# First loads handed to three DMA queues in another order, and matmuls on constants placed ahead of the first data

## The chip, the cores and the metric

The kernel runs on one core of a Trainium2 chip. A core has a matrix engine (TensorE, in the profile PE, with its weight loads as PEld), a vector engine (VectorE, DVE), a scalar engine (ScalarE, ACT), a general engine (GpSimd, POOL) and a sync engine (SyncE, SP) that issues most transfers. The metric is the device time of one launch in microseconds: the median of several runs, 953.85 us over 4 runs (952.91 to 955.61).

## The reference

A linear attention without softmax, normalised per head, feeds a two-layer network with a gated activation. All is float32 in value (the two weight matrices arrive as float64 and are converted in the kernel).

```python
# q, k, v: (8 batches, 8 heads, 576 tokens, 64); g_norm: (64,)
kv  = einsum('bhsd,bhse->bhde', k, v)            # one 64x64 matrix per head
out = einsum('bhsd,bhde->bhse', q, kv)
rms = sqrt(mean(out * out, axis=-1) + 1e-6)
x   = (out / rms * g_norm)  ->  (4608 tokens, 512)
h   = x @ w_in                                   # (512, 2048)
g   = h * erf(softplus(h))
result = g @ w_out                               # (2048, 512)
```

## The kernel before

**Tiles and stages.** Each of the 8 batches T has 576 tokens: 512 of them form one tile of 128 x 512, the remaining 64 of all eight batches together form a ninth tile. The 8 heads of a batch are handled as 4 pairs p = 0..3, two heads of 64 side by side in 128 partitions. The attention of a pair is a list of pieces that the main program places one by one: `products` (k and v of the pair give `kv_ps` on PE in 12 small matmuls, the last tokens' q, `q_last`, are transposed for every second pair, DVE copies `kv_ps` into `bd_kv`, PE transposes the four q blocks into `qt_ps`, ACT copies them out), `apply` (two matmuls with `bd_kv`, one for the last tokens and one for the 512; DVE copies `x_last`, ACT squares), `mean` (a matmul with the constant `mean_w`, then logarithm, exponential and square on ACT) and `norm` (three DVE operations that end in `xT`).

**The first stage.** Batch 0 has nothing before it to hide behind. Its four pairs run as a small software pipeline, written out by hand: in round i, `products` of pair i, `apply` of pair i-1, `norm` of pair i-3, `mean` of pair i-2. Into the same rounds go the conversions of the first weight pieces: `load` brings a raw float64 piece (`w_raw`), `split` and `join` turn it into float32 with five DVE and two ACT operations (`w_e`, `w_m`, then `w_in_sb` or `w_out_sb`). After that come the first hidden-layer matmuls (`h_ps`), and from there the attention of batch T+1 is woven into the network of batch T. The first two batches use plain float32 matmuls; from the end of batch 1 on, weights and activations are cut into three parts each (`n_ps`, `m_ps` matmuls), the cut weights are stored to memory and read back, and that is most of the run.

**Queues.** Every engine works through its own instructions in program order. Transfers are issued by instructions in three such queues: SP's, ACT's and POOL's. SP's and ACT's issues take eight completion semaphores in turn; an issue that comes round to a semaphore again waits until the transfer that had it eight places earlier has landed. POOL's issues have semaphores of their own.

**The first loads.** `load_pair(i)` issues q of a pair from SP, and k and v from `side`, which is ACT for pairs 0 to 2 and SP from then on. A q load moves 256 KB, a k or v load of batch 0 288 KB. `load_last(T, p)` issues 32 KB, the last 64 tokens' q of a pair, from SP. On SP the order is: q of pair 0, last q of pairs 0 and 1, q of pairs 1 and 2, two raw weight pieces of 512 KB, last q of pairs 2 and 3, then q, k and v of pair 3, then two more weight pieces. On ACT: k and v of pairs 0, 1 and 2. On POOL: the two halves of `g_col` (g_norm), then the identity matrix and the zeroing of `bd_kv`. `gm_col`, computed from `g_col` on POOL, is read first by the last operation of `norm`.

**PE's order at the start.** `products(0)`, `products(1)`, `apply(0)`, `products(2)`, `apply(1)`, `mean(0)`, `products(3)`, `apply(2)`, `mean(1)`, `apply(3)`, `mean(2)`, `mean(3)`, then 16 matmul passes of `h_ps`. On DVE, between the copy of `bd_kv` of pair 1 and that of pair 2 stand the two first operations of the first weight piece, and between those of pair 2 and pair 3 the rest of that piece and the two first operations of the second.

Of the kernel before, what the change touches and what calls it, by code (L numbers as in the profile page):

```python
# [39 lines left out]
FP32 = mybir.dt.float32  # L40
# [20 lines left out]
def kernel(  # L61
# [10 lines left out]
    nc = tc.nc  # L72
    P = 128
    B, H, S, D = q.shape
    DM, DF = moe_w_in.shape[0], moe_w_in.shape[1] // 2
    J = 4
    G = J * P
    R = S - G
    NP = H // 2
# [5 lines left out]
    const = ctx.enter_context(tc.tile_pool(name="const", bufs=1))  # L85
# [12 lines left out]
    ps_o = ctx.enter_context(tc.tile_pool(name="ps_o", bufs=1, space=PSUM))  # L98
# [12 lines left out]
    q_sb, k_sb, v_sb = {}, {}, {}  # L111
# [4 lines left out]
    def chunks(T):  # L116

        return 6 if T == 0 else 5

    def load_pair(i):  # L120
        T, p = divmod(i, NP)
        if T >= B:
            return
        pool = early if i in (2, 3) else kvp
        side = nc.scalar if i < 3 else nc.sync
        t = q_sb[T, p] = pool.tile([P, J, 2, D], FP32, name="q_sb", tag="q")
        nc.sync.dma_start(
            out=t, in_=q[T, 2 * p : 2 * p + 2, 0:G, :].rearrange("h (p j) d -> p j h d", j=J)
        )
        for name, got, src in (("k", k_sb, k), ("v", v_sb, v)):  # L130
            C = chunks(T)
            rows, rest = divmod(S, C)
            assert rest < 2
            t = got[T, p] = pool.tile([rows + rest, 2, C, D], FP32, name=f"{name}_sb", tag=name)
            heads = src[T, 2 * p : 2 * p + 2]
            side.dma_start(  # L136
                out=t[:rows].rearrange("r h c d -> r h (c d)"),
                in_=heads[:, : S - rest].rearrange("h (r c) d -> r h (c d)", c=C),
            )
            if rest:  # L140
                side.dma_start(
                    out=t[rows:, :, 0], in_=heads[:, S - rest :].rearrange("h r d -> r h d")
                )

    def load_last(T, p):
        if T < B:
            nc.sync.dma_start(
                out=q_last[p % 2 * R : p % 2 * R + R, p // 2],
                in_=q[T, 2 * p : 2 * p + 2, G:S, :].rearrange("h r d -> r h d"),
            )  # L150

    g_col = const.tile([P, 1], FP32, name="g_col")
    for i in range(2):
        nc.gpsimd.dma_start(
            out=g_col[i * D : i * D + D, :], in_=g_norm.rearrange("(d one) -> d one", one=1)
        )
    for i in range(NP - 1):
        load_pair(i)
        if i == 0:
            load_last(0, 0)  # L160
            load_last(0, 1)

    w_in_sb = first_w.tile([P, KC, DF], FP32, name="w_in_sb")
    w_out_sb = first_w.tile([P, FC, DM], FP32, name="w_out_sb")
# [1 line left out]

    ident = const.tile([P, P], FP32, name="ident")
    make_identity(nc, ident)
    mean_w = const.tile([P, P], FP32R, name="mean_w")
    mean_f = early.tile([P, P], FP32, name="mean_f", bufs=1)  # L170
    nc.vector.memset(mean_f, 0.0)
# [4 lines left out]
    nc.vector.memset(exp_col, -896.0 * (1 << 23))  # L176
    eps_col = const.tile([P, 1], FP32, name="eps_col")
    nc.vector.memset(eps_col, EPS)
    bd_kv = const.tile([P, 2, P], FP32, name="bd_kv")
    nc.gpsimd.memset(bd_kv, 0.0)  # L180
    gm_col = const.tile([P, 1], FP32, name="gm_col")
    nc.gpsimd.tensor_scalar(out=gm_col, in0=g_col, scalar1=-0.5, scalar2=None, op0=ALU.mult)
    x_last = const.tile([P, KC, G], FP32, name="x_last")
# [66 lines left out]
    def w_next(what):  # L250
        i = w_at[what]
        if i < len(w_order):
            w_at[what] = i + 1
            {"load": load_w, "split": w_split, "join": w_join}[what](*w_order[i][1:])
# [14 lines left out]
    def attention(T, p, pools=None):  # L269
# [18 lines left out]
        def products():  # L288
# [17 lines left out]
            if p == NP - 2:  # L306
                for i in range(NP):
                    load_last(T + 1, i)
# [82 lines left out]
        def loads():  # L391
            load_pair(T * NP + p + 2)
# [156 lines left out]
    def unit(name):  # L549
        return gate.tile([P, G], FP32, name=name, tag=name[0])  # L550


    for _ in range(2):
        w_next("load")
    load_last(0, 2)
    load_last(0, 3)
    load_pair(NP - 1)

    w_rounds = {
# [4 lines left out]
        6: ("split", "join", "load", "join", "load"),  # L564
    }
    banks_0 = {"kv_ps": (ps_at, "at"), "qt_ps": (ps_h, "h"), "ms_ps": (ps_h, "h")}
    first = [attention(0, p, banks_0 | {"se_ps": (ps_o, f"o{p}")}) for p in range(NP)]
    for i in range(NP + 3):
        for piece, p in ((0, i), (1, i - 1), (4, i - 3), (3, i - 2)):
            if 0 <= p < NP:  # L570
                first[p][piece]()
        if i == 1:
            for _ in range(RAW - 2):
                w_next("load")
            load_pair(NP)
            load_pair(NP + 1)
        for what in w_rounds.get(i, ()):
            w_next(what)
# [65 lines left out]
    for n in range(FIRST * FC + 1):  # L644
        T, f = divmod(n, FC)
# [33 lines left out]
        elif T < FIRST:  # L679
# [10 lines left out]
            for i, c in blocks:  # L690
                nc.tensor.matmul(  # L691
                    plain[i],
                    lhsT=w_in_sb[:, c, i % FC * P : i % FC * P + P],
                    rhs=xT[T][:, c, :],
                    start=(c == 0),
                    stop=(c == KC - 1),
                )
        if T < FIRST:
            if n == whole:
                old_h = acc.tile([P, BATCH, G], FP32, name="h", tag="e")  # L700
            h = hs[n] = old_h[:, n - whole] if n >= whole else unit("h_sb")
# [51 lines left out]
    def part(h, half):  # L753
        return h[:, :, half * 2 * P : half * 2 * P + 2 * P]
# [31 lines left out]
    for m in range(first_batch, batches + 1):  # L786
        T, b = divmod(m, NB)
        todo = []
        if T + 1 < NG:
            todo = list(attention(T + 1, b))  # L790
            if b == 0:
                side = late_r if T % 2 == FIRST % 2 else late
# [28 lines left out]
        if m < batches:  # L821
            h = wide.tile([P, BATCH, G], FP32, name="h", tag="h")
# [22 lines left out]
        for j in range(J):  # L845
# [7 lines left out]
            for half in range(2) if j == 1 and m < batches - 1 else (j,) if j < 2 and m == batches - 1 else ():  # L853
                nc.vector.tensor_tensor(  # L854
                    out=part(h, half), in0=part(h, half), in1=part(s, half), op=ALU.mult
# [38 lines left out]
```

## Time and profile before

| | |
|---|---|
| median of 4 runs | 953.85 us (952.91 to 955.61) |
| the run that was profiled | 955.61 us, of which the span of the core's instructions is 953.8 us |
| mean granted PE clock in it | 0.996 |
| PE busy | 929.7 us, 97% of the span |
| DVE busy | 740.7 us, 78% |
| ACT busy | 615.8 us, 65% |
| POOL busy | 2.4 us in 10 instructions |
| moved by DMA | 259.78 MB, mean 272 GB/s |
| chain that ended last | PE 82%, DVE 6%, ACT 5%, DMA 4%, SP's queue 2% |
| PE busy from 0 to 10 us, 10 to 20, 20 to 30, 30 to 40, 40 to 50 | 2.46, 7.67, 8.48, 9.29, 10.00 us |

How to read it: the profile is one execution. A busy PE is a PE with a matmul in flight, which says nothing about its clock. The chain that ended last is followed back from the last instruction, each time to whatever released the instruction; "DMA" in it is the time from the issue of a transfer to its landing. The whole run is bound by PE, but PE is not the bound in the first 40 us, as the rows above show, and that is where the change lies.

### The profile page before, as it was taken

How to read it: one execution, taken by the hardware profiler on the slowest of the kernel's cores; microseconds unless marked ns; L12 is line 12 of the kernel's file. 1: busy time of each engine (PE TensorE's matmuls, PEld its weight loads, DVE VectorE, ACT ScalarE, POOL GpSimd, SP SyncE). 2: the span in 40 equal slices, each digit the busy share in tenths (PEclk: the TensorE clock that was granted, in tenths of full speed). 3: DMA queues.
4: the chain of work that ended last, by engine and by line, in shares of the span. 5: the costliest groups of instructions: out<-in, count | busy, mean ns of one | idle time of the engine just before them, and what ended most of it. 6: DMA issues, size and time to landing. Idle time of an engine off the chain costs nothing.

```text
span 953.8 us, 11746 instructions
## 1 busy us (share of the span) xinstructions
PE 929.7 (97%) x4272; PEld 685.7 (72%) x4272; DVE 740.7 (78%) x1054; ACT 615.8 (65%) x825; POOL 2.4 (0%) x10
## 2 busy tenths in 40 slices
PE   5999999999998999999999999999999999999998
PEld 3444445665686888888888888888888788878886
DVE  3979958888575888888888888877887877777667
ACT  3889866777664666666666666666666666665552
POOL 1000000000000000000000000000000000000000
PEclk9999999999998999999999999999999999999999
DMA  9756505899699888998889889988897778768872
GB/s 250 267 165 215 174 10 214 308 343 337 215 344 336 274 279 287 306 309 296 287 309 314 298 292 306 325 292 286 278 341 260 263 252 352 282 248 307 333 275 64
DMA packets 111842, 259.78 MB, mean 272 GB/s; under 512 B 43864, under 2 KB 69544, under 8 KB 111784
## 3 DMA queue, kind: packets, MB, share of 16 engines
q1 hardware_dynamic: 110152, 256.73, 77.5%
q10 hardware_dynamic: 1568, 2.29, 0.9%
q8 instruction: 34, 0.56, 0.2%
q14 instruction: 24, 0.20, 0.1%
q0 software_dynamic: 64, 0.00, 0.0%
HBM read 224.40 MB, written 34.60 MB: 272 GB/s over the span
## 4 chain that ended last, share of the span: by engine, by line
PE 82%; DVE 6%; ACT 5%; DMA 4%; SPq 2%; issue 1%; DVEq 0%
PE n_ps L462 42%; PE m_ps L462 21%; PE o_ps L520 8%; PE h_ps L691 3%; PE se_ps L325 2%; PE kv_ps L297 2%; PE qt_ps L319 1%; DMA w_raw<-in_moe_w_in_dram 1%; DMA out_dram<-e 1%; DMA w_in_parts<-w_in 1%; SPq L136 1%; ACT w_e L215 1%; ACT w_m L219 1%; DMA v_sb<-in_v_dram 1%; PE ms_ps L347 1%
## 5 line engine op out<-in xcount | busy, mean ns | idle before, releaser
L462 PE MATMUL n_ps<-x_forms,w_in_parts 128*128 128x512 f32 x896 | 235.1, 404 | 5.4 <-ACT h L834 3.8
L462 PE MATMUL n_ps<-w_out_parts,g_forms 128*128 128x512 f32 x928 | 231.6, 392 | 0.0
L462 PEld LDWEIGHTS n_ps<-x_forms,w_in_parts 128*128 128x128 f32 x896 | 167.8, 189 | 49.7 <-issue 9.3
L462 PEld LDWEIGHTS n_ps<-w_out_parts,g_forms 128*128 128x128 f32 x928 | 174.6, 188 | 38.6 <-issue 1.7
L836 ACT ACTIVATE s<-h 128x512 f32<-128x512 f32 x112 | 71.1, 635 | 179.5 <-DVE h L445 179.5
L445 DVE TENSOR_TENSOR h<-m_ps,h 128x512 f32<-128x512 f32 x116 | 79.8, 688 | 68.6 <-ACT h L834 49.2
L462 PE MATMUL m_ps<-w_out_parts,g_forms 128*128 128x512 f32 x464 | 124.2, 390 | 0.0
L462 PE MATMUL m_ps<-x_forms,w_in_parts 128*128 128x512 f32 x448 | 120.8, 392 | 0.0
L520 PE MATMUL o_ps<-w_out_sb,h_sb 128*128 128x512 f32 x224 | 100.8, 593 | 0.3 <-DVE h_sb L642 0.3
L462 PEld LDWEIGHTS m_ps<-w_out_parts,g_forms 128*128 128x128 f32 x464 | 87.1, 188 | 18.1
L462 PEld LDWEIGHTS m_ps<-x_forms,w_in_parts 128*128 128x128 f32 x448 | 84.7, 189 | 17.8
L445 DVE TENSOR_TENSOR e<-m_ps,e 128x512 f32<-128x512 f32 x116 | 80.3, 692 | 18.2 <-PE m_ps L462 10.9
L440 DVE SCALAR_TENSOR_TENSOR e<-n_ps,e 128x512 f32<-128x512 f32 x88 | 60.4, 686 | 38.3 <-PE n_ps L462 38.2
L520 PEld LDWEIGHTS o_ps<-w_out_sb,h_sb 128*128 128x128 f32 x224 | 42.4, 190 | 48.8 <-issue 46.6
L834 ACT ACTIVATE h<-n_ps 128x512 f32<-128x512 f32 x112 | 65.5, 585 | 13.9 <-DMA w_in_parts<-w_in 10.0
L411 DVE SCALAR_TENSOR_TENSOR g_forms<-g_forms 128x1024 fp32r<-128x1024 f32 x58 | 71.1, 1225 | 2.0
L408 DVE TENSOR_TENSOR g_forms<-h,g_forms 128x1024 fp32r<-128x1024 f32 x58 | 70.6, 1218 | 1.7 <-ACT g_forms L405 1.4
L405 ACT ACTIVATE g_forms<-h 128x1024 fp32r<-128x1024 f32 x58 | 58.9, 1060 | 12.4 <-PE m_ps L462 9.8
L854 DVE TENSOR_TENSOR h<-h,s 128x1024 f32<-128x1024 f32 x56 | 66.0, 1218 | 0.7 <-ACT s L840 0.7
L691 PE MATMUL h_ps<-xT,w_in_sb 128*128 128x512 f32 x144 | 64.9, 595 | 0.8 <-DVE w_in_sb L240 0.6
L106 ACT ACT_TABLE_LOAD x44 | 56.5, 1283 | 0.7
L840 ACT ACTIVATE s<-s 128x1024 f32<-128x1024 f32 x56 | 56.3, 1052 | 0.3
(98 smaller groups left out, 1014.3 us busy)
## 6 DMA issues: line engine op xcount, KB each, us to landing
w_out_parts<-w_out SPq DMA_DIRECT2D x116, 768.0 KB
w_in_parts<-w_in SPq DMA_DIRECT2D x112, 768.0 KB
w_in<-w_new SPq DMA_DIRECT2D x16, 768.0 KB
q_sb<-in_q_dram SPq DMA_DIRECT2D x32, 256.0 KB
w_raw<-in_moe_w_out_dram SPq DMA_DIRECT2D x8, 1024.0 KB
out_dram<-e SPq DMA_DIRECT2D x32, 256.0 KB
k_sb<-in_k_dram SPq DMA_DIRECT2D x28, 287.5 KB
v_sb<-in_v_dram SPq DMA_DIRECT2D x28, 287.5 KB
```

The source lines that it names most:

```text
L106: nc.scalar.preload_act_table_set("softplus")
L405: nc.scalar.activation(high, x, AF.Copy, scale=1.0 + 2.0**-13)
L408: nc.vector.tensor_tensor(out=low, in0=x, in1=high.bitcast(FP32), op=ALU.subtract)
L411: nc.vector.scalar_tensor_tensor(out=both, in0=low.bitcast(FP32), scalar=SHIFT, in1=high.bitcast(FP32), op0=ALU.mult, op1=ALU.add,)
L440: nc.vector.scalar_tensor_tensor(out=out_, in0=ps, scalar=scale, in1=out_, op0=ALU.mult, op1=ALU.add)
L445: nc.vector.tensor_tensor(out=out_, in0=ps, in1=out_, op=ALU.add)
L462: nc.tensor.matmul(ps, lhsT=weights(form, k), rhs=moving(form, k), start=(form == forms[0] and k == 0), stop=(form == forms[-1] and k == 3),)
L520: nc.tensor.matmul(o_ps[j], lhsT=g[:, j * P : j * P + P], rhs=w_out_sb[:, f, :], start=(f == 0), stop=last,)
L691: nc.tensor.matmul(plain[i], lhsT=w_in_sb[:, c, i % FC * P : i % FC * P + P], rhs=xT[T][:, c, :], start=(c == 0), stop=(c == KC - 1),)
L834: nc.scalar.activation(h[:, i], n_ps, AF.Copy, scale=SHIFT - 1.0)
L836: nc.scalar.activation(s[:, i], h[:, i], AF.Softplus)
L854: nc.vector.tensor_tensor(out=part(h, half), in0=part(h, half), in1=part(s, half), op=ALU.mult)
```

## The change

The order and the queues of the first nine k, v and q loads are written out in a list; q of the last tokens of batch 0 goes to POOL's queue, all four at once, behind the identity and the zeroing of `bd_kv` and ahead of `g_col`; 8 matmuls of 128 x 128 on constants (`mean_w`, `mean_f`) are put ahead of the first `products` on PE, and 4 more between `products(0)` and `products(1)`. They write a PSUM tile `idle` that nothing reads, in the bank that `apply(3)` uses later.

```diff
-    def load_pair(i):
-        T, p = divmod(i, NP)
-        if T >= B:
-            return
-        pool = early if i in (2, 3) else kvp
-        side = nc.scalar if i < 3 else nc.sync
-        t = q_sb[T, p] = pool.tile([P, J, 2, D], FP32, name="q_sb", tag="q")
-        nc.sync.dma_start(
+    def load_part(i, name, side=nc.sync):
+        T, p = divmod(i, NP)
+        pool = early if i in (2, 3) else kvp
+        if name == "q":
+            t = q_sb[T, p] = pool.tile([P, J, 2, D], FP32, name="q_sb", tag="q")
+            side.dma_start(
...
+    def load_pair(i):
+        if i < B * NP:
+            for name in "qkv":
+                load_part(i, name)
+
-    def load_last(T, p):
+    def load_last(T, p, side=nc.sync):
         if T < B:
-            nc.sync.dma_start(
+            side.dma_start(
...
+    for i, name, side in (
+        (0, "k", nc.sync),
+        (0, "v", nc.scalar),
+        (0, "q", nc.sync),
+        (1, "k", nc.scalar),
+        (1, "v", nc.scalar),
+        (1, "q", nc.sync),
+        (2, "k", nc.sync),
+        (2, "v", nc.sync),
+        (2, "q", nc.sync),
+    ):
+        load_part(i, name, side)
...
+    ident = const.tile([P, P], FP32, name="ident")
+    make_identity(nc, ident)
+    bd_kv = const.tile([P, 2, P], FP32, name="bd_kv")
+    nc.gpsimd.memset(bd_kv, 0.0)
+    for i in range(NP):
+        load_last(0, i, nc.gpsimd)
     g_col = const.tile([P, 1], FP32, name="g_col")
     for i in range(2):
         nc.gpsimd.dma_start(
             out=g_col[i * D : i * D + D, :], in_=g_norm.rearrange("(d one) -> d one", one=1)
         )
-    for i in range(NP - 1):
-        load_pair(i)
-        if i == 0:
-            load_last(0, 0)
-            load_last(0, 1)
...
     for _ in range(2):
         w_next("load")
-    load_last(0, 2)
-    load_last(0, 3)
     load_pair(NP - 1)
...
+    idle = ps_o.tile([P, P], FP32, name="idle", tag="o3")
+
+    def keep_warm(n):
+        for _ in range(n):
+            nc.tensor.matmul(idle, lhsT=mean_w.bitcast(FP32), rhs=mean_f, start=True, stop=True)
+
+    keep_warm(8)
     first = [attention(0, p, banks_0 | {"se_ps": (ps_o, f"o{p}")}) for p in range(NP)]
     for i in range(NP + 3):
         for piece, p in ((0, i), (1, i - 1), (4, i - 3), (3, i - 2)):
             if 0 <= p < NP:
                 first[p][piece]()
+        if i == 0:
+            keep_warm(4)
```

More of the change, by code (lines that the diff above doesn't have):

```diff
@@ L118, in chunks @@
         return 6 if T == 0 else 5
-    def load_pair(i):
+    def load_part(i, name, side=nc.sync):
         T, p = divmod(i, NP)
-        if T >= B:
-            return
         pool = early if i in (2, 3) else kvp
-        side = nc.scalar if i < 3 else nc.sync
-        t = q_sb[T, p] = pool.tile([P, J, 2, D], FP32, name="q_sb", tag="q")
-        nc.sync.dma_start(
-            out=t, in_=q[T, 2 * p : 2 * p + 2, 0:G, :].rearrange("h (p j) d -> p j h d", j=J)
-        )
-        for name, got, src in (("k", k_sb, k), ("v", v_sb, v)):
+        if name == "q":
+            t = q_sb[T, p] = pool.tile([P, J, 2, D], FP32, name="q_sb", tag="q")
+            side.dma_start(
+                out=t, in_=q[T, 2 * p : 2 * p + 2, 0:G, :].rearrange("h (p j) d -> p j h d", j=J)
+            )
+        else:
+            got, src = (k_sb, k) if name == "k" else (v_sb, v)
             C = chunks(T)
@@ L150, in load_last @@
             )
+    for i, name, side in (
[10 more added lines that the diff above has]
+        load_part(i, name, side)
+    w_in_sb = first_w.tile([P, KC, DF], FP32, name="w_in_sb")
+    w_out_sb = first_w.tile([P, FC, DM], FP32, name="w_out_sb")
+    ident = const.tile([P, P], FP32, name="ident")
[4 more added lines that the diff above has]
+        load_last(0, i, nc.gpsimd)
     g_col = const.tile([P, 1], FP32, name="g_col")
@@ L156 @@
         )
-    for i in range(NP - 1):
-        load_pair(i)
-        if i == 0:
-            load_last(0, 0)
-            load_last(0, 1)
[L163 to L168, printed above, removed]
     mean_w = const.tile([P, P], FP32R, name="mean_w")
@@ L178 @@
     nc.vector.memset(eps_col, EPS)
-    bd_kv = const.tile([P, 2, P], FP32, name="bd_kv")
-    nc.gpsimd.memset(bd_kv, 0.0)
     gm_col = const.tile([P, 1], FP32, name="gm_col")
```

## The prediction

> **What bounds the kernel now.** I first read the chain of waits of the whole run. It is PE for 82%, and nothing of the change touches a steady-state matmul, so only the start can change. Then the same chain for the first 60 us:
>
> ```profile
> 4.35 11.44 DMA w_raw<-in_moe_w_in_dram
> 15.79 0.02 issue
> 15.81 5.43 DMA v_sb<-in_v_dram
> 21.24 0.14 issue
> 21.38 0.92 PE kv_ps L297 x24
> ...
> 38.47 0.69 DVE w_in_sb L240
> 39.16 0.61 DVE w_e L207
> ```
>
> Columns are start, length, what. Until 21.24 the end waits for transfers: v of pair 3, the last of the first loads. From there to 39.8 it is PE for 1.5 us and then DVE without a gap, then ACT, then PE. I call the landing of that v "T". Is DVE itself late, whatever T is? Its timeline (start, length, engine, line, idle before):
>
> ```profile
> 18.82 0.46 DVE L312 COPY bd_kv<-kv_ps 64x64 f32<-64x64 f32 x2 [2.24 <-PE kv_ps L305]
> ...
> 22.38 0.45 DVE L312 COPY bd_kv<-kv_ps 64x64 f32<-64x64 f32 x2
> 23.09 0.23 DVE L326 COPY x_last<-kv_ps 128x64 f32<-128x64 f32 x1 [0.26 <-PE kv_ps L324]
> ```
>
> From the copy of pair 2 (18.82) to that of pair 3 (22.38) DVE has 3.56 us of work and almost no gap, and pair 3's data allow that copy at 21.24 + 0.14 + 0.92 = 22.30. So two paths meet there: T, and the copy of pair 2, which itself waited for the last tokens' q. Both must move if the end is to move. Third, the transfers in stretches (the numbers behind the bracketed counts are the clock, the DMA share and GB/s):
>
> ```profile
> 2.00:4.00 2.00, 0.00 (x0) 0.00 (x0) 0.00 (x0) 0.00 (x1) 1.22 (x4) 1.00 1.04 288
> 4.00:6.00 2.00, 0.00 (x0) 0.00 (x0) 0.00 (x0) 0.00 (x0) 0.00 (x0) 1.00 0.55 162
> 6.00:8.00 2.00, 1.38 (x24) 1.39 (x24) 0.00 (x0) 0.00 (x0) 0.00 (x0) 1.00 1.05 244
> 8.00:10.00 2.00, 1.08 (x9) 0.93 (x5) 0.32 (x2) 0.00 (x0) 0.21 (x1) 1.00 1.15 286
> 10.00:12.00 2.00, 0.39 (x2) 0.00 (x0) 0.42 (x2) 0.58 (x1) 0.00 (x0) 1.00 1.09 244
> ```
>
> The DMA engines are full from 2 us on (share 1.03 to 1.22 up to 24 us), except from 4 to 6 us, at half. T is set by bytes over rate, with one hole. Last, PE's timeline:
>
> ```profile
> 6.62 1.55 PE L297 MATMUL kv_ps<-v_sb,k_sb 96*64 96x64 f32 x24 [6.62 <-DMA v_sb<-in_v_dram]
> 9.09 0.45 PE L305 MATMUL kv_ps<-ident,q_last 128*128 128x128 f32 x1 [0.92 <-DMA q_last<-in_q_dram]
> 9.33 1.06 PE L319 MATMUL qt_ps<-ident,q_sb 128*128 128x128 f32 x4
> 12.38 1.55 PE L297 MATMUL kv_ps<-v_sb,k_sb 96*64 96x64 f32 x24 [1.99 <-DMA v_sb<-in_v_dram]
> ...
> 21.38 0.92 PE L297 MATMUL kv_ps<-v_sb,k_sb 96*64 96x64 f32 x24 [0.20 <-DMA v_sb<-in_v_dram]
> ```
>
> The same 24 passes take 1.55 us twice and 0.92 us at 21.38: PE is slow until about 17 us, though the stretches print a clock of 1.00 there.
>
> **The loads.** Nothing is removed: the four pairs (8 x 288 KB and 4 x 256 KB), the last tokens' q (128 KB) and two weight pieces (1 MB) still stand ahead of v of pair 3, 4.6 MB. What can change is the hole. It is worth 2 us x (1.08 - 0.55) = 1.06 us of full engines, 1.08 being near the share of the stretches beside it. Around it the queues hold little: two 32 KB loads on SP behind the first q (1.33 us of issue for 64 KB), and on ACT the issue of v of pair 1, held to 5.57 us by its semaphore, that of the first q. Afterwards SP issues k0, q0, q1, k2, v2, q2 (by their rows 0.40 + 0.78 + 0.62 + 0.40 + 0.40 + 0.70 = 3.3 us, so by 4.0 us; the sixth waits for k0, which landed at 3.64) and ACT v0, k1, v1 with no wait. So 288 or 256 KB stand behind every issue and the hole should fill. Bounds: nothing (the hole is the start-up of the queues and stays) and 1.3 us (it fills and the last q's 0.65 us issues also cost nothing). I take 1.05 us: T at 20.2.
>
> A page of the Trainium skill speaks against this. The row is share 0.55 at 4 to 6 us with two queues in use. "DMA: Bandwidth & Descriptors", Issuing engines are not separate DMA queues, says that all queues run on the same 16 engines and that using more of them saves only issue time, usually small. The full stretches agree (1.05 to 1.15 with two queues); the hole does not show full engines. By the rule taken strictly the gain would be 0 and the sum 953.85; by the row it is 1.05.
>
> **POOL's queue.** Before, its two `g_col` issues began at 1.23 and took 1.23 us together, landing after:
>
> ```profile
> DMA to landing us min/median/max: 5.0/5.4/5.9
> ```
>
> Identity and zeroing (0.24 + 0.29 + 0.31 us of work) now go first, so the four loads issue from about 2.1 us, some 0.65 us each, and the first two land at 2.1 + 5.0 = 7.1 and, 1.7 us apart as the two `g_col` landings were (gm_col starts at 8.04, the first landed at 1.23 + 5.0 = 6.2), at 8.8. These rows are of 64 elements of 4 bytes, ours are 128 of 256 bytes: below, 0.65 us apart (7.8); above, twice 1.7 (10.5). I take 8.8, nearest the row; the old one came at 9.0. The last two land then at 10.5 and 12.2 (above: 17.3) against an old need at 18.4. `g_col` comes by 13 to 21 us and is first needed at 24.79 minus 1: hidden by all of batch 0's attention; later than that it would hold DVE one for one.
>
> **PE's constant matmuls.** Two passes each. A 512-column matmul (L325) took 2.02 us slow and 1.08 fast, a quarter of it 0.50 and 0.27. The first 8: 2.2 to 4.0 us, beginning at 1.65 when `mean_w` is cast, so done by 5.7 in a wait that lasted to 6.62; if k and v came at 4 they would delay them by 1.7 us, but PE then waits for last q at 8.8 anyway. The 4 others, 1.1 to 2.0 us, stand behind the transposes of q0. Queued behind them: `products(1)`, `apply(0)`, `products(2)`. Their chain, from the last-q transposes to the copy of pair 2, by rows at the old speed: 0.45 + 1.06 + (1.1 to 2.0) + kv and transposes of pair 1 2.5 + apply 2.14 + kv of pair 2 1.10 + 0.34 = 8.7 to 9.6 us. From 8.8 the copy stands at 17.5 to 18.4; the T path needs it at 18.82 - 1.05 = 17.77. At the fast rates (0.92 for 1.55, 0.62 for 1.06, 1.08 for 2.02) it takes about 6 us and is hidden in the transfers. So at slow speed up to 0.6 us of the gain is lost; I charge 0.05, since some of it will run fast.
>
> "TensorE: Matmul & The Clock Gate", Part 1, says that the PE clock is halved until some 3.4 us of sustained activity. The row 1.55 against 0.92 agrees with two speeds. By the rule the filler buys the fast rate before the first pair; by the rows the price of the slow rate is off the path, 0 either way, unless last q is late.
>
> **The sum.** -1.05 + 0.05 = -1.0 us. After T the same DVE, ACT and PE work follows. Transfers do not swallow the shift later: the DMA share is 0.09 from 60 to 70 us and 0.65 from 240 to 260. The profiled execution, span 953.8 in a run of 955.61, would become 952.8 in 954.6; that run is 1.76 above the median, so I take the median: 953.85 - 1.0 = **952.8 us**. A reserve of doubt: from 285.6 to 294.4 ACT waits 10.0 us for cut weights and the clock is 0.52 from 294 to 301; if that gap lands differently, a run moves by up to half of those 7 us x 0.48, 1.7 us, either way.
>
> **The rivals.**
> *More than the hole.* The order changes the mix of long and short packets. If the 4.6 MB flow at the 302 GB/s of the stretch 12 to 14 (15.2 us) instead of the 263 that is the mean from 2 to 21.3 us (17.5 us), T falls by 2.3 us; DVE, whose first weight piece comes earlier by as much, follows if PE is fast: 951.5. For: idle DVE of 2.24 and 3.52 us ahead of 18.82. Against: full engines already.
> *Nothing.* The hole is start-up and moves along; PE's filler is off the path: 953.8. For: the first packets are of any order. Against: ACT's held issue.
> *POOL late (the slower side).* The place is the transpose of the last q in `products(0)`; PE is in order, so all pairs queue behind. From a landing at 18.82 - 9.6 = 9.2 to 10.1 on, each us costs one. With the above bound 10.5: 954.2 to 955.1; at 13 us: 18.82 becomes 21.7 to 22.6, 956.7 to 957.6. For: the only loads whose price no row shows. Against: 5.0 to 5.9 us for landings measured on that queue.
>
> **How the numbers follow.** Forecast 0.40, more 0.30, nothing 0.12, POOL late 0.18. The likeliest's own range is 951.7 to 953.9. 0.2% (1.9 us) is about what a measurement of this kernel can tell from no change. Faster by over that: all of "more" and a fifth of the forecast, 0.38. Slower: 0.14 of POOL late. The rest, 0.48, within. The range 950.5 to 955.4 leaves 0.08 below and 0.12 above.
>
> **What would show it.** Right: DMA share near 1.05 from 4 to 6 us; v of pair 3 landing near 20.2, its kv at 20.3; last-q transpose of pair 0 near 9; DVE's copy of pair 3 near 21.3 and DVE without a gap after it; kv of pair 1 at under 1.55 us. Wrong: a hole that stays, a T that has not moved, or a copy of pair 2 after 18.8 with PE waiting for last q.

## The result and the profile after

The change makes the kernel a little faster: median 951.75 us (37 runs, 950.7 to 955.81) against 954.03 us before (58 runs), a ratio of 0.9981 with a 95% interval of 0.9976 to 0.9985, that is 1.4 to 2.3 us (the medians differ by 2.28). 952.8 us was predicted, 1.05 us below the median then known. Ratios count only the runs within 1.5% of the fastest of their kernel, which leaves out 2 of the 6 runs of the cut kernel before and 3 of the 6 of the cut change further down; medians count all. The profiled execution has a span of 949.8 us in a run of 951.57.

The chain of waits of the changed kernel from 0 to 60 us (start, length, what):

```profile
10.40 2.15 SPq L125
12.55 0.04 issue
12.60 1.00 SPq L135
13.60 0.04 issue
13.64 5.85 DMA v_sb<-in_v_dram
19.49 0.14 issue
19.62 0.92 PE kv_ps L311 x24
...
36.66 0.69 DVE w_in_sb L254
37.35 0.61 DVE w_e L221
```

From T on it is the same chain as before, with v of pair 3 landing (T) at 19.49 in place of 21.24, and DVE's `w_e` at 37.35 in place of 39.16. The 1.8 us gained at T is still there at 39 us. Ahead of T it differs: before, the issue of that v waited until 15.81 for the first raw weight piece, which landed at 15.79; now it stands at 13.64, behind the issues ahead of it on SP's queue. At the copies of `bd_kv` on DVE (start, length, engine, line, idle before) pair 2 and pair 3 have both moved:

```profile
16.45 0.46 DVE L326 COPY bd_kv<-kv_ps 64x64 f32<-64x64 f32 x2 [0.92 <-PE kv_ps L319]
...
20.58 0.46 DVE L326 COPY bd_kv<-kv_ps 64x64 f32<-64x64 f32 x2 [0.50 <-PE kv_ps L311]
```

Pair 2 was copied at 18.82 and pair 3 at 22.38. DVE now even waits 0.50 us for pair 3, so T alone sets the end here. The stretches (after the bracketed counts: clock, DMA share, GB/s):

```profile
2.00:4.00 2.00, 2.00 (x11) 2.00 (x11) 0.00 (x0) 0.01 (x1) 2.00 (x4) 1.00 0.81 253
4.00:6.00 2.00, 1.66 (x11) 1.40 (x12) 0.00 (x0) 0.00 (x0) 1.10 (x3) 1.00 1.12 249
...
10.00:12.00 2.00, 2.00 (x11) 2.00 (x10) 0.73 (x3) 0.58 (x1) 0.22 (x1) 0.50 1.14 255
12.00:14.00 2.00, 2.00 (x32) 1.71 (x32) 0.30 (x2) 0.00 (x0) 0.00 (x0) 0.80 1.13 345
```

The hole from 4 to 6 us is gone (0.55 to 1.12). A smaller one came from 2 to 4 us (1.04 to 0.81). Last, PE:

```profile
1.68 3.78 PE L584 MATMUL idle<-mean_f,mean_w 128*128 128x128 f32 x16 [1.68 <-DVE eps_col L194]
5.80 0.98 PE L311 MATMUL kv_ps<-v_sb,k_sb 96*64 96x64 f32 x24 [0.34 <-DMA v_sb<-in_v_dram]
9.74 0.45 PE L319 MATMUL kv_ps<-ident,q_last 128*128 128x128 f32 x1 [2.96 <-DMA q_last<-in_q_dram]
...
10.83 1.92 PE L584 MATMUL idle<-mean_f,mean_w 128*128 128x128 f32 x8
12.68 0.96 PE L311 MATMUL kv_ps<-v_sb,k_sb 96*64 96x64 f32 x24
```

The constants run in the first wait as planned and the kv passes of pair 0 are fast (0.98 us). Then PE waits 2.96 us for the last tokens' q from POOL's queue, which comes at 9.74 against 9.09 before, and the clock falls again: the stretch 10 to 12 us has 0.50.

Not all that these two profiles differ by is the change. From 295 us on their distance is not 1.8 but 3.6 to 4.0 us, because both wait near 290 us and the clock was low for 7 us behind that wait before, for 3.4 us after. The median and the interval, not the two spans, tell the gain.

### The profile page after: what moved, and what is told of

Same layout as the page of the kernel before. It is cut to its first block, busy times and chain, and to the rows that moved or that the text cites. A ratio compares the mean times of both kernels' runs of the same rounds, so it can differ in the third digit from the quotient of the medians.

```text
span 949.8 us, 11799 instructions
## 1 busy us (share of the span) xinstructions
PE 931.6 (98%) x4296; PEld 688.3 (72%) x4296; DVE 740.7 (78%) x1054; ACT 615.9 (65%) x825; POOL 4.7 (0%) x14
## 4 chain that ended last, share of the span: by engine, by line
PE 83%; DVE 6%; ACT 6%; DMA 2%; issue 1%; SPq 1%; DVEq 0%; ACTq 0%
PE n_ps L476 43%; PE m_ps L476 21%; PE o_ps L534 8%; PE h_ps L713 3%; PE se_ps L339 2%; PE kv_ps L311 2%; PE qt_ps L333 1%; DMA out_dram<-e 1%; DMA q_sb<-in_q_dram 1%; DVE h L876 1%; ACT w_e L229 1%; ACT L103 1%; DVE h L459 1%; DMA v_sb<-in_v_dram 1%; ACT w_m L233 1%
```

## The experiments

### The parts, in the whole kernel

Four kernels each hold a part of the change.

`no_warm`: the change without `idle` and `keep_warm`.

```diff
-    keep_warm(8)
...
-        if i == 0:
-            keep_warm(4)
```

> The whole change without the twelve constant matmuls. Theory 1 (the transfers give the gain: v of pair 3 lands at 19.5 in place of 21.2 us, and PE's clock is off the path): it lands at 19.4 to 19.8 here too, DVE's copy of pair 3 stands at 20.6 to 21.1, and the kernel is 1.3 to 1.8 us faster than before. Theory 2 (the fast PE is what lets DVE use the earlier data): PE's work on pairs 0 to 2 takes 8.7 us from the last-q transposes as in the old rows, the copy of pair 2 comes after 18, that of pair 3 after 22, and the kernel is 0 to 0.6 us faster than before.

Measured: 952.55 us, ratio 0.9991 (0.9981 to 1.0), 0 to 1.8 us faster. Its own profile has kv of pair 3 at 19.88 and the copies of pairs 2 and 3 at 17.25 and 20.83, though PE stays slow until 16 us. T and the copies are where theory 1 had them; the time, 0.9 us by the ratio and 1.4 by the medians, does not part the theories.

`warm_only`: the kernel before with `idle`, `keep_warm(8)` and `keep_warm(4)` at the places of the change.

> The kernel before with the twelve constant matmuls alone. Theory 1: v of pair 3 lands at 21.0 to 21.4 as before and the time is the same within 0.4 us. Theory 2: 0.8 to 1.8 us faster.

Measured: 952.4 us, ratio 0.999 (0.9979 to 1.0). That looked like theory 2, but its profile does not. PE's lines of it:

```profile
6.05 0.92 PE L297 MATMUL kv_ps<-v_sb,k_sb 96*64 96x64 f32 x24 [0.61 <-DMA v_sb<-in_v_dram]
...
10.98 1.55 PE L297 MATMUL kv_ps<-v_sb,k_sb 96*64 96x64 f32 x24 [0.47 <-DMA v_sb<-in_v_dram]
...
19.56 0.92 PE L297 MATMUL kv_ps<-v_sb,k_sb 96*64 96x64 f32 x24 [0.24 <-DMA v_sb<-in_v_dram]
```

With the old loads, kv of pair 3 starts at 19.56 here and at 21.38 in the profile before, both times waiting for the landing of v, and none of the issues ahead of that v waits for a matmul. So T scatters by more than 1 us from one profile to the next, and the one profile of before was a late one. The pairs in between were no faster for it (pair 1 takes 1.55 us: the clock was down again).

`last_on_pool`: the kernel before with the last tokens' q of batch 0 on POOL's queue, and POOL's own order, alone.

```diff
-            load_last(0, 0)
-            load_last(0, 1)
...
+    for i in range(NP):
+        load_last(0, i, nc.gpsimd)
```

> The kernel before with the last tokens' q of batch 0 on POOL's queue (behind identity and zeroing, as in the change) and nothing else: k and v of pairs 0 to 2 stay on ACT, q on SP. Theory 1 with the hole from 4 to 6 us laid to small loads in front of big ones: the DMA share there rises from 0.55 to 0.8 or more, v of pair 3 lands 0.5 to 1.0 us earlier, 0.4 to 1.0 us faster. If the hole is ACT's held issue or the order of k, v and q: share stays under 0.65 and the time within 0.3 us of before.

Measured: 956.38 us, ratio 1.0029 (1.0018 to 1.004): slower by 1.7 to 3.8 us. The hole did fill (share 1.01 from 4 to 6 us), so the small loads do make it, yet the time went up. From its timelines of ACT's queue, PE and DVE:

```profile
10.40 0.32 ACTq L136 DMA_DIRECT2D v_sb<-in_v_dram  x1
```

```profile
16.60 1.55 PE L296 MATMUL kv_ps<-v_sb,k_sb 96*64 96x64 f32 x24 [1.05 <-DMA v_sb<-in_v_dram]
18.08 0.48 PE L304 MATMUL kv_ps<-ident,q_last 128*128 128x128 f32 x1
```

```profile
18.59 0.46 DVE L311 COPY bd_kv<-kv_ps 64x64 f32<-64x64 f32 x2 [3.92 <-PE kv_ps L304]
...
22.75 0.46 DVE L311 COPY bd_kv<-kv_ps 64x64 f32<-64x64 f32 x2
```

The issue of v of pair 2 stands on ACT until 10.40 (8.98 before): with four loads fewer in the round of eight semaphores its turn fell to that of q of pair 1. The weights went ahead of it. PE got pair 2 at 16.60, still at the slow rate, DVE idled 3.92 us, and pair 3 was copied at 22.75 although nothing on PE waited for its data. By the completion records of its trace v of pair 3 had landed at 19.45, as early as in the changed kernel: T came early, and the path through the copy of pair 2 lost the time.

`order_only`: the new order and queues of k, v and q; last q on SP at its old places; no constants.

> The new order and queues of k, v and q, with the last tokens' q on SP at its old places and no constant matmuls. If the order of the large loads gives the gain: share at 4 to 6 us above 0.9, v of pair 3 at 19.5 to 20.2, 0.9 to 1.8 us faster than before. If the small loads on SP make the hole: share stays near 0.6 and the gain is under 0.5 us.

Measured: 956.37 us, ratio 1.0031 (1.0017 to 1.0044), slower too. SP's queue and PE in it:

```profile
5.21 1.91 SPq L135 DMA_DIRECT2D k_sb<-in_k_dram  x1
8.85 0.31 SPq L135 DMA_DIRECT2D v_sb<-in_v_dram  x1
```

```profile
18.51 0.30 PE L320 MATMUL kv_ps<-ident,q_last 128*128 128x128 f32 x1 [1.97 <-DMA q_last<-in_q_dram]
...
22.86 0.92 PE L312 MATMUL kv_ps<-v_sb,k_sb 96*64 96x64 f32 x24
```

With the last q still in the round, v of pair 2 comes back to the semaphore of q of pair 0 and holds SP's queue until 8.85; everything behind it is late: the DMA share falls to 0.90 from 12 to 14 us, the other last q land after 18, v of pair 3 lands at 21.24 and its kv starts at 22.86. The hole at 4 to 6 us is filled here as well (1.11) and no gain comes of it.

### The start by itself

The later stages scatter by more than the parts differ. So four kernels, and later a fifth, stop after five hidden tiles of batch 0; they leave out all that follows and store one hidden tile.

```diff
-    for n in range(FIRST * FC + 1):
+    for n in range(5):
...
+    nc.gpsimd.dma_start(out=out[0:P, :], in_=hs[4])
```

> The kernel before, cut off after five hidden tiles of batch 0 and with one of them stored as the only output, so that the scatter of the later stages is gone. The whole is some 55 to 70 us; this is the base for the three beside it, and its own runs show how much the start scatters: I expect 1 to 2 us from lowest to highest.

> The change, cut at the same place (the later stages and all other output left out). If the gain of the whole kernel is made in the start: 1.4 to 2.2 us less than the cut kernel before.

> The loads of the change without the constant matmuls, cut at the same place. Additive theory (loads 0.9, constants 1.0 of the 1.8): 0.6 to 1.2 us less than the cut kernel before. My first theory (the loads are all of it): within 0.3 us of the cut change.

> The constant matmuls alone on the old loads, cut at the same place. Additive theory: 0.6 to 1.4 us less than the cut kernel before. First theory: the same within 0.3 us.

The fifth is the cut `no_warm` with pair 2 on ACT:

```diff
-        (2, "k", nc.sync),
-        (2, "v", nc.sync),
+        (2, "k", nc.scalar),
+        (2, "v", nc.scalar),
```

> Cut kernel, loads of the change without constants, but k and v of pair 2 on ACT behind v of pair 1, as in the kernel before. If the eight turns of the semaphores and the small loads are what counts (v of pair 2 then waits for q of pair 0 alone): within 0.4 us of the cut kernel with them on SP (60.3 us). If need order in one queue is what counts (weights now run beside pair 2): 0.7 to 2 us slower, first raw weight piece earlier, v of pair 2 later than 12 us.

| cut kernel | median, lowest to highest, us | ratio to the whole kernel before (95%) |
|---|---|---|
| before | 61.64, 60.90 to 62.03 (6 runs) | 0.0644 (0.0641 to 0.0647) |
| change | 60.40, 59.42 to 62.59 (6) | 0.0628 (0.0625 to 0.0631) |
| loads without constants | 60.29, 59.83 to 60.70 (4) | 0.0633 (0.0630 to 0.0635) |
| constants on the old loads | 62.03, 61.42 to 62.18 (4) | 0.0650 (0.0647 to 0.0652) |
| loads, pair 2 on ACT, no constants | 60.11, 59.78 to 60.61 (4) | 0.0631 (0.0628 to 0.0634) |

One unit in the fourth decimal is 0.095 us. The loads alone are worth 1.35 us by the medians and 1.05 by the ratios. The constants on the old loads cost 0.4 to 0.6 us; on the new ones they are worth nothing by the medians (-0.1) and 0.5 us by the ratios. That kernel's runs spread over 3.2 us against 0.9 without them, so the half us rests on which of its runs are counted. My first theory, the loads, holds by the medians and is not settled by the ratios; the additive one falls on the cut `warm_only`. Pair 2 on ACT is as good as on SP: its v waits there for q of pair 0 (issue at 7.97), as in `order_only`, but on ACT no other load stands behind that wait. So here it did not matter which of the two queues carries pair 2, and a held issue with nothing behind it cost nothing.

The hole comes back in every profile with the old loads (a share of 0.55 to 0.65). The stretch of the cut kernel before, and that of the cut loads without constants:

```profile
4.00:6.00 2.00, 0.00 (x0) 0.00 (x0) 0.00 (x0) 0.00 (x0) 0.00 (x0) 1.00 0.61 160
```

```profile
4.00:6.00 2.00, 0.90 (x17) 0.93 (x19) 0.00 (x0) 0.00 (x0) 1.03 (x2) 1.00 1.14 288
```

### Again, and a filler at another place

`after_again` is the change once more.

> The change once more, as the base for the two with filler at 290 us: 1.3 to 2.3 us faster than before, v of pair 3 landing at 18.5 to 20, and one or two slow-clock windows of 3.4 us after the wait at 290 us.

Measured: 951.53 us, ratio 0.9982 (0.9972 to 0.9991), the first result again; kv of pair 3 at 19.42. Near 290 us PE waited 1.84 us, and this time the clock stayed at 1.00 behind it.

`gap_fill` tries to better the change where both kernels wait near 290 us.

```diff
+            spare["ps"] = kv_ps
...
+            if m == first_batch + 1 and i == 3:
+                for _ in range(12):
+                    nc.tensor.matmul(
+                        spare["ps"][:, 3 * P : 4 * P],
+                        lhsT=mean_w.bitcast(FP32),
+                        rhs=mean_w.bitcast(FP32),
+                        start=True,
+                        stop=True,
+                    )
```

> The change with twelve more matmuls on constants in PE's wait at 290 us (2.0 to 3.9 us in the six full profiles so far), written to unused columns of a bank in use. If the slow clock that follows this wait is paid in full (3.4 us at half clock, 1.7 us lost), the clock stays at 1.00 from 285 to 305 and the kernel is 1 to 2 us faster than the change, 2.8 to 3.8 us faster than before. If what follows the wait is held by something else: same as the change within 0.5 us, or up to 0.8 us slower where the wait is short.

Measured: 958.65 us, ratio 1.0056 (1.0044 to 1.0069): slower by 4.2 to 6.6 us than before. PE's timeline:

```profile
288.55 1.07 PE L477 MATMUL m_ps<-x_forms,w_in_parts 128*128 128x512 f32 x4
295.82 5.49 PE L850 MATMUL kv_ps<-mean_w 128*128 128x128 f32 x24 [6.20 <-DVE x_last L341]
300.96 2.37 PE L477 MATMUL n_ps<-x_forms,w_in_parts 128*128 128x512 f32 x8
```

The filler waited itself. It writes the bank that DVE's copy of `x_last` reads, and that copy stands in DVE's order behind the very work that is late. A wait of about 2 us became 6.20, the clock fell, and the 24 passes then took 5.49 us at the slow rate in front of the real work.

`gap_fill_no_warm` is that without the constants at the start.

> The same filler at 290 us, without the twelve constant matmuls at the start. If the start needs only the loads (the cut kernels: 60.3 us without constants, 60.4 with them, 61.6 before), it is within 0.5 us of the kernel with both; if the constants at the start earn 1 us, it is 0.7 to 1.2 us slower than that.

Measured: 959.5 us, ratio 1.0065 (1.0052 to 1.0078), the same fault (6.70 us of wait). Its interval and that of `gap_fill` overlap, so it does not settle what the constants at the start earn. Whether a filler that waits for nothing would help at 290 us was not tried. No run beats the change.

## Why the prediction was right

**The bound and the two paths.** Right: T and pair 2's copy met at 22.4, both moved, and the rest followed unchanged through DVE and ACT.

**The loads, -1.05 us.** Right in mechanism and in size: the hole filled (1.12 where 1.05 was named), and by itself the start gains 1.05 to 1.35 us from the loads. In the two first profiles T moved by 1.75 us. A part of that is the late profile of before: kv of pair 3 starts on the old loads at 21.38, 19.56, 19.91 and 20.11 (mean 20.24, in the profiles of before, `warm_only` and the cut kernels before and with constants), with the change's loads at 19.62, 19.42, 19.88, 18.57 and 19.07 (mean 19.31; change, again, `no_warm`, cut change, cut without constants). That is 0.9 us, or 0.8 with the two profiles that have the change's loads and a filler at 290 us (19.76 and 19.50). What the hole has to do with it can be read from the transfers up to T, in the first two profiles (clock, DMA share and GB/s stand last):

```profile
0.00:21.24 21.24, 11.30 (x96) 7.74 (x96) 5.01 (x21) 5.39 (x9) 2.39 (x10) 1.00 0.95 240
```

```profile
0.00:19.49 19.49, 13.81 (x120) 11.02 (x120) 5.66 (x22) 5.91 (x9) 4.71 (x14) 0.91 1.01 259
```

Both moved some 5 MB before that v was there (240 GB/s over 21.24 us, 259 over 19.49), the first at a mean share of 0.95, the second at 1.01. The other profiles agree: 0.94 to 0.96 up to T in all four with the old loads, 1.00 to 1.01 in all with the change's, and 4.9 to 5.1 MB in every one. As an estimate, this difference of some 0.055 of a full share over 19.5 us is 1.1 us, the price of the hole. What scatters beside it is the rate at the same share, 240 to 255 GB/s with the old loads. In the two first profiles the transfers of 12 to 20 us also moved more, 2.64 MB against 1.91 + 0.31 on two queues, at about the same share; whether the new order gives that, as the rival "more" had it, the runs do not show.

**The reason I gave.** Incomplete. I wrote that 288 or 256 KB behind every issue fill the hole. They do in `last_on_pool` and in `order_only` too, and these lose 2.8 and 3.0 us by the ratios. In `last_on_pool` T came early with the filled hole (19.45, a share of 0.99 up to there), and the copy of pair 2 was late. In `order_only` the share fell again behind SP's held issue (0.94 up to the landing at 21.24). I priced the order and POOL's queue as terms that add; each alone costs, together they gain. In both traces the loss starts at an issue that waits for an earlier load in the round of eight; no run changes those waits alone. They could be read off the kernel before, and I used them for one issue only. Nor were SP's six issues done by 4.0 us: that of k of pair 2 alone took 3.73 us, from 2.74, and v and q of the pair were issued at 6.51 and 7.25. Why it took that long the runs do not show.

The Trainium skill's "DMA: Bandwidth & Descriptors", Issuing engines are not separate DMA queues, says that more queues save only issue time. The full stretches bear that out, 1.03 to 1.24 whatever the queues. As a forecast of 0 it missed, because the engines were not full in the hole: with the last q on POOL's queue, v of pair 1 was issued at 2.31 in `last_on_pool` and at 1.70 in the change, where the round of semaphores had held it until 5.57.

**POOL's queue.** Issue was 2.56 us for four, 0.64 each (0.65 predicted), from 1.49 us (2.1). The first two were wanted on PE at 9.74 (8.8 predicted, 9.09 before), and `gm_col` was made at 11.08, long before its need. The slower rival stayed away: pair 2's copy came at 16.45, at slow rates in `no_warm` at 17.25, against 17.5 to 18.4 predicted and 17.77 needed.

**The constants, +0.05 us.** Sizes right: 3.78 us for eight (2.2 to 4.0) and 1.92 for four (1.1 to 2.0). That their clock is off the path holds only while T is late. By the completion records, v of pair 3 landed at 18.06 in the cut kernel without constants, and PE, still at the slow rate for pair 2 (1.55 us), came to its kv only at 19.07, without a wait; in the cut change it landed at 18.44 and kv started at 18.57. That is 0.5 us for the constants, as by the ratios, in one profile of each. In the whole kernel it stays open: 0.9981 with them and 0.9991 without, with intervals that overlap.

**The sum.** -1.0 predicted, -1.8 measured (-1.4 to -2.3). At the start the loads measured what they were priced at, so what is over comes from the constants or from behind the start. From kv of pair 3 to the end the change took 930.2 us, and 929.9 in `after_again`; the kernel before, `warm_only` and `no_warm` took 932.4, 931.7 and 931.8. PE's wait near 290 us was 2.01 and 1.84 us in the first two, 3.85, 3.59 and 3.67 in the others. That is the place that the prediction held in reserve (ACT's 10.0 us of wait there end at 294.4, so they begin at 284.4 and not at 285.6). Whether the change shortens that wait or these five executions fell so, the runs do not part.

## What to carry to other kernels

Where issues share a few completion semaphores in turn, a load moved from one queue to another changes what every later issue waits for; write down for each issue which earlier landing it needs, for the whole new order, before pricing any part. Do not judge the parts of such a reordering one by one: here two that lose 2.8 and 3.0 us make a gain together. A filler for an idle engine must depend on nothing that is itself late, its output bank's readers included.

## What the runs showed of the hardware

The constants buy little time at the fast clock. In the changed kernel the kv passes of pair 0 took 0.98 us after 3.78 us of constants (1.50 in `after_again`, after the same 3.78), but the stretch from 10 to 12 us, behind a wait of 2.96 us, has a granted clock of 0.50; `warm_only` shows 0.50 from 10 to 14 us. "TensorE: Matmul & The Clock Gate", Part 1, gives a window of some 3.4 us for both directions, and waits shorter than that were punished here: after 2.0 us near 290 us the stretch 290 to 295 stands at 0.77 in the change, while after 1.84 us it stayed at 1.00 in `after_again`. In the first 17 us of the kernel before, the same passes took 1.55 us under a printed clock of 1.00: there the durations, not the printed clock, tell the rate.
